# A four-layer recurrent-memory / hedgehog-attention kernel: feature weights multiplied into the query and key weights on the chip

## The chip, the cores and the metric

The kernel runs on one core of one Trainium2 chip. The metric is the device time in microseconds; the time given for a kernel is the median of its runs. Every detailed duration below comes from one profiled execution on that core, counted from the start of its span.

## What is computed

Two layer types alternate, A B A B, over an activation of 2048 rows by 640 columns. Layer A is a recurrent-memory attention over 64 segments of 32 rows; the change doesn't touch its mathematics. Layer B is a linear attention with 32 heads of 20 columns and a "hedgehog" feature map:

```python
qkv = (x @ wqkv)                       # x: normalised rows, 640 -> 3 x 640
q, k, v = ...                          # 32 heads, 20 columns each
pq = einsum('bhsd,hdf->bhsf', q, w_phi)
pk = einsum('bhsd,hdf->bhsf', k, w_phi)
phi_q = concat(softmax(pq), softmax(-pq))
phi_k = concat(softmax(pk), softmax(-pk))
kv = einsum('bhsf,bhsd->bhfd', phi_k, v)
z  = einsum('bhsf->bhf', phi_k)
num = einsum('bhqf,bhfd->bhqd', phi_q, kv)
den = einsum('bhqf,bhf->bhq', phi_q, z) + 1e-06
x = x + (num / den) @ wo
```

Both B layers use the same `wqkv`, `w_phi` and `wo`.

## The kernel before

**Layer A** (lines 582 to 1149) has a preparation (`A_pre`), in which TensorE (PE) works at full rate, and a chain of 64 segments (`A_chain`), each depending on the one before. Its instructions are ordered by hand. After the chain, `post_steps` multiplies the attention outputs of the last 8 rows of every segment by Wo, in four batches of 96 matmuls (`multiply`). Layer B's code calls it.

**Layer B** (`layer_B`, lines 249 to 550) is placed by a scheduler that works at build time: it decides the order of the instructions on each engine, and each engine then runs its own list in that order. An instruction whose inputs aren't ready blocks everything behind it on its engine. Layer B has these stages:

- *Start* (456 to 474). SP issues the loads of x, of the tail outputs and of the three 640-column parts of `wqkv`, in the order keys (j = 1), values (2), queries (0). The four `multiply` batches run on PE while the first rows are normalised (`norm_rows`, line 357: an addition on POOL, statistics on DVE, logarithm and exponential on ACT, scaling). `turn_rows` transposes normalised rows on PE into `xnT` and ACT copies them out of PSUM.
- *Loop* (476 to 489) over NG = 4 groups of 512 rows. `heads_T(xnT, 1, "kT")` computes the keys of the group, columns on partitions: six chunks of six heads (120 columns; the sixth has 40), each the sum of five matmuls of 512 columns. Each chunk is copied from PSUM to SBUF, five by ACT and the last by DVE. `keys_values` then takes the group's four blocks of 128 rows. For a block it multiplies the keys by `wbd`, a block-diagonal form of `w_phi` (seven small matmuls into two PSUM banks), takes exp and exp of the negative on ACT (line 407), sums them per head (410) and inverts the sums (412) on DVE. It computes the values with two times five matmuls of 320 columns (419), scales them on DVE (423) and adds to the running kv sums with twelve small matmuls (429). At the end of the group `heads_T(xnT, 0, "qT")` does for the queries what was done for the keys.
- `query_features` of a group runs one group later, and for the last group in the tail: six matmuls with `wbd` (439), twelve exponentials on ACT (441), twelve matmuls that sum them per head (445), reciprocals, and twelve times a spreading matmul (452) with a multiplication on DVE (453).
- *Tail* (490 to 550): masked copies of kv and its sums, then per group denominators, numerators, the output projection (533) and, in the first B layer, the next normalisation.

Ten names of PSUM tiles share a pool of three banks (`bank`, line 297). A second pool of two (`side_bank`) holds those of the query features and denominators. `late_constants` (317) fills constants on POOL and DVE and is placed at the second group's normalisation.

The loop, the part that the change rewrites most:

```python
keys_values(g, xnT)
if waiting is not None:
    query_features(*waiting)
waiting = (g, heads_T(xnT, 0, "qT"))
```

All large buffers are cut by hand from one `arena`. Addresses under LATE = 64512 hold in layer B among others `qTs`, `lgs`, `oTs`, `obs`; above it lie `wbd`, `wqkv`, `kTs`, `xnTs`, `vrs`, `x2`, `xns`. In layer A the same addresses hold weights, so that a load of A's weights waits for the B buffers that it overlaps.

## Time and profile before

| what | us |
|---|---|
| median of 3 runs (3726.93 to 3730.69) | 3728.3 |
| span of the profiled execution | 3735.3 |
| layer B, first time: first key matmul to first numerator | 1617.1 to 1777.5 |
| layer B, second time: first key matmul to first numerator | 3487.2 to 3643.2 |
| second layer A: first matmul of its preparation | 1881.7 |
| DMA of one 640-column part of `wqkv`, from issue to landing | 10.7 |

Over the whole span PE is busy 3543.7 us (95%), DVE 2368.0 (63%), ACT 2073.4 (56%) and POOL 1658.5 (44%). Most of that is layer A: its chain runs from about 169 to 1555 and from about 2045 to 3430. In the profile's rows PE means matmuls and PEld the loading of their stationary operand. "Idle before, releaser" says how long an engine stood before an instruction and what it waited for. Matmuls overlap in the pipeline, so the time that one more of them costs is the distance between starts, not the duration in its row: for the 512-column matmul the row says 379 ns, and thirty in a row start within 6.67 us, 222 ns apart.

### The profile page before, as it was taken

What the parts mean: (1) busy time and instruction counts of PE and PEld (TensorE: products, weight loads), DVE (VectorE), ACT (ScalarE), POOL (GpSimd) and SP (SyncE); (2) the same over time, 40 slices, a digit from 0 to 9 for tenths busy, and PEclk for the clock granted to TensorE, in tenths of its full rate; (3) what the DMA queues carried; (4) which work ended last, traced back from release to release, by engine and by line L of the source; (5) the groups of instructions that cost most, each with busy time, mean ns of one, the idle gap of its engine ahead of it and who ended that gap; (6) DMA issues with size and microseconds to landing.
All of it is one profiled execution on the core that took longest, in us unless ns stands there. A gap on an engine that the chain in (4) does not pass through costs nothing.

```text
span 3735.3 us, 169098 instructions
## 1 busy us (share of the span) xinstructions
PE 3543.7 (95%) x71082; PEld 2319.9 (62%) x71390; DVE 2368.0 (63%) x6330; ACT 2073.4 (56%) x5285; POOL 1658.5 (44%) x4323
## 2 busy tenths in 40 slices
PE   9999999999999999989899999999999999999898
PEld 7766666666666666545377666666666666665453
DVE  5556666666666666456633566666666666664564
ACT  2356566666666666545423566666666666665453
POOL 3345555555555555340423455455555555553400
PEclk9999999999999999989899999999999999999899
DMA  9988788888887888910377888887887888879100
GB/s 301 326 295 294 266 289 292 275 291 278 284 294 272 293 282 276 309 57 14 137 259 216 292 279 282 283 295 275 290 282 274 289 282 289 293 268 316 58 1 29
DMA packets 531381, 931.72 MB, mean 249 GB/s; under 512 B 141034, under 2 KB 298362, under 8 KB 530618
## 3 DMA queue, kind: packets, MB, share of 16 engines
q1 hardware_dynamic: 428794, 818.87, 62.6%
q0 software_dynamic: 68160, 88.78, 8.1%
q10 hardware_dynamic: 33664, 13.24, 1.4%
q8 instruction: 558, 9.14, 1.0%
q14 instruction: 205, 1.68, 0.1%
HBM read 852.43 MB, written 72.09 MB: 248 GB/s over the span
## 4 chain that ended last, share of the span: by engine, by line
PE 35%; DVE 5%; DMA 5%; ACT 4%; issue 4%; POOL 2%; PEld 2%; SPq 0%; POOLq 0%; DVEq 0%; ACTq 0%
PE ps_qk L926 9%; PE ps_w L1002 4%; PE ps_v L926 4%; PE ps_o L976 2%; PE ps_s L968 2%; PE ps_qk L389 2%; DMA arena<-wo_rows 2%; PE ps_pre L817 1%; PE ps_s L1034 1%; DVE hT L882 1%; PEld L817 1%; PE ps_s L963 1%; PE ps_idle L1009 1%; PE ps_v L419 1%; PE kv L429 1%
## 5 line engine op out<-in xcount | busy, mean ns | idle before, releaser
L926 PEld LDWEIGHTS <-hT 128*32 128x32 bf16 x30720 | 739.4, 96 | 433.1 <-DVE hT L1146 29.0
L926 PE MATMUL ps_qk<-arena,hT 128*32 128x384 bf16 x20480 | 996.3, 327 | 12.0 <-DMA arena<-in_A_Wk_dram 2.2
L936 ACT ACTIVATE raw<-ps_qk 128x384 bf16<-128x384 f32 x1024 | 503.1, 491 | 378.3 <-PE ps_s L1034 243.9
L1002 PE MATMUL ps_w<-arena,OT 128*32 128x160 bf16 x24576 | 542.7, 235 | 38.4 <-issue 22.1
L909 POOL DMA_DIRECT2D Vp<-vb x512 | 258.8, 506 | 661.6 <-PE ps_o L976 456.4
L926 PE MATMUL ps_v<-arena,hT 128*32 128x384 bf16 x10240 | 536.6, 329 | 6.6 <-DMA arena<-in_A_Wv_dram 6.6
L1002 PEld LDWEIGHTS <-OT 128*32 128x32 bf16 x24576 | 436.2, 97 | 131.1 <-issue 53.7
L941 DVE STREAM_TRANSPOSE KT<-raw 128x384 bf16<-128x384 bf16 x512 | 296.1, 578 | 195.9 <-ACT raw L936 191.9
L944 DVE STREAM_TRANSPOSE QT<-raw 128x256 bf16<-128x256 bf16 x512 | 227.9, 445 | 239.1 <-ACT raw L936 195.9
L897 POOL DMA_DIRECT2D kqb<-kqb x512 | 291.1, 569 | 173.3 <-POOL KT L905 148.2
L957 DVE CAST Vp<-ps_v 64x384 bf16<-64x384 f32 x512 | 286.2, 559 | 98.2 <-ACT Vp L955 82.7
L995 POOL DMA_DIRECT2D otb<-otb x512 | 283.0, 553 | 116.5 <-DVE otb L991 99.0
L955 ACT ACTIVATE Vp<-ps_v 64x384 bf16<-64x384 f32 x512 | 246.3, 481 | 154.2 <-PE ps_v L926 115.4
L982 DVE CAST OT<-ps_o 128x192 bf16<-128x192 f32 x512 | 183.2, 358 | 221.2 <-PE ps_o L976 203.1
L1041 DVE TENSOR_TENSOR E<-E,ps_s 80x320 bf16<-80x320 bf16 x512 | 247.5, 483 | 73.6 <-ACT ps_s L1040 69.5
L1020 ACT ACTIVATE E<-ps_s 80x320 bf16<-80x320 f32 x512 | 221.9, 433 | 126.1 <-PE ps_s L968 97.2
L976 PEld LDWEIGHTS <-Vp 80*128 80x128 bf16 x4096 | 184.3, 99 | 154.7 <-issue 120.6
L968 PE MATMUL ps_s<-QT,KT 128*80 128x80 bf16 (+1 forms) x3072 | 233.2, 213 | 24.3 <-DVE KT L941 13.4
L976 PE MATMUL ps_o<-E,Vp 80*128 80x80 bf16 x4096 | 234.5, 202 | 22.6 <-ACT Vp L955 4.2
L981 ACT ACTIVATE OT<-ps_o 128x192 bf16<-128x192 f32 x512 | 167.8, 328 | 152.6 <-PE ps_o L976 152.3
L890 ACT ACTIVATE Vp<-ps_w 32x160 bf16<-32x160 f32 x512 | 150.7, 294 | 175.0 <-DVE wt L1145 157.9
L968 PEld LDWEIGHTS <-KT 128*80 128x80 bf16 x3072 | 194.6, 119 | 73.5 <-issue 61.4
(152 smaller groups left out, 5462.5 us busy)
## 6 DMA issues: line engine op xcount, KB each, us to landing
arena<-wo_rows SPq DMA_DIRECT2D x792, 320.0 KB, 6.8
arena<-in_A_Wq_dram SPq DMA_DIRECT2D x427, 384.0 KB, 4.6
arena<-in_A_Wv_dram SPq DMA_DIRECT2D x427, 384.0 KB, 6.4
arena<-in_A_Wk_dram SPq DMA_DIRECT2D x768, 192.0 KB, 4.8
kqb<-kqb POOLq DMA_DIRECT2D x512, 48.0 KB, 5.1
arena<-in_A_Wk_dram SPq DMA_DIRECT2D x43, 384.0 KB, 7.1
vb<-arena POOLq DMA_DIRECT2D x128, 112.0 KB, 5.9
Vp<-vb POOLq DMA_DIRECT2D x512, 28.0 KB, 4.7
```

What stands on the lines that cost most here:

```text
L897: nc.gpsimd.dma_start(out=kqb[:], in_=self.kqb_d[s, :, r, :])
L909: nc.gpsimd.dma_start(out=Vs[n % 2][64:80, :], in_=self.vb_d[s, r].rearrange("g t f -> (g t) f"))
L926: nc.tensor.matmul(o[32 * g:32 * g + 32, 0:384], lhsT=hT[:, b, :], rhs=rhs, start=(i == 0), stop=(i == KC - 1), tile_position=(0, 32 * g), ...
L936: nc.scalar.activation(out=raw[:], in_=ps[:, 0:384], func=ACT.Copy)
L941: nc.vector.transpose(out=KT[:, :, 0:64], in_=raw[:, :].rearrange("p (c j) -> p c j", j=64))
L955: nc.scalar.activation(out=o, in_=i, func=ACT.Copy)
L957: nc.vector.tensor_copy(out=o, in_=i)
L968: nc.tensor.matmul(S[0:80, c0:c0 + 80 * (q1 - q0)], lhsT=KT[:, 3 * x + i, :], rhs=QT[:, x, q0:q1, :], start=False, stop=(x == 1 and i == 2 ...
L976: nc.tensor.matmul(O[x][:, 80 * i:80 * i + 80], lhsT=Vs[n % 2][0:80, 448 * x + k:448 * x + k + 128], rhs=E[0:80, 160 * x + 80 * e:160 * x ...
L995: nc.gpsimd.dma_start(out=self.otb_d[s, :, 96 * r:96 * r + 96], in_=otb[:, :, :].rearrange("p c t -> p (c t)"))
L1002: nc.tensor.matmul(W[32 * g:32 * g + 32, 0:160], lhsT=OT[:, c, q:q + 32], rhs=w[:, 640 * i + 160 * g:640 * i + 160 * g + 160], start=(firs ...
L1041: nc.vector.tensor_tensor(out=E[0:80, 0:320], in0=E[0:80, 0:320], in1=rc, op=ALU.mult)
```

## The change

The product (rows x Wq) x w_phi is computed as rows x (Wq x w_phi), and the same for the keys. A new function `fuse` makes the product of the weights on the chip in the first B layer, between the last `multiply` and the loop, and writes it over the query and key parts of `wqkv`. A DMA on POOL's queue keeps it in DRAM (`fused_d`), and the second B layer loads it from there in place of the raw weights. In the loop the key features then come from `xnT` directly, five matmuls of 320 columns for each half of a block; query features from the former query matmuls, with the exponentials reading their PSUM banks. `heads_T` is gone, and with it its copies and the buffers `qTs` and `kTs`. A smaller `wT` takes the place of `kTs`, which moves the buffers behind them. The features of a group's queries now belong to their own group; what is left of `query_features`, the normalisation, is `query_norms` and stays where it was.

```diff
-        qTs = self.views(take(2 * f4), f4, 2)
...
-        kTs = self.views(take(2 * f4), f4, 2)
+        wT = self.view(take(KC * NC_ * 256), KC * NC_ * 256).rearrange("p (k c m) -> p k c m", k=KC, c=NC_)
...
-            def heads_T(xnT, j, name):
...
+            def fuse(j):
+                for k in range(KC):
+                    pt = bank("ps_t", BF16)
+                    for c in range(NC_):
+                        self.transp(out=pt[0:sizes[c], P * c:P * c + P],
+                                    in_=wqkv[:, k, D * j + CH * c:D * j + CH * c + sizes[c]], identity=self.ident[:, :])
+                    full = P * (NC_ - 1)
+                    self.ev.copy(out=wT[0:CH, k, 0:NC_ - 1, :].rearrange("p c m -> p (c m)"), in_=pt[0:CH, 0:full])
+                    self.ev.copy(out=wT[0:sizes[-1], k, NC_ - 1, :], in_=pt[0:sizes[-1], full:full + P])
+                for k in range(KC):
+                    for c0, c1 in ((0, 3), (3, NC_)):
+                        ps = bank("ps_f")
+                        for c in range(c0, c1):
+                            mc, o = sizes[c], CH * (c - c0)
+                            nc.tensor.matmul(ps[:, o:o + mc], lhsT=wT[0:mc, k, c, :], rhs=wbd[0:mc, c, 0:mc], start=True,
+                                             stop=True)
+                        n = sum(sizes[c0:c1])
+                        self.ev.copy(out=wqkv[:, k, D * j + CH * c0:D * j + CH * c0 + n], in_=ps[:, 0:n])
+                nc.gpsimd.dma_start(out=self.fused_d[:, :, D * j:D * j + D], in_=wqkv[:, :, D * j:D * j + D])
 
             def keys_values(g, xnT):
-                kT = heads_T(xnT, 1, "kT")
...
-                        for c in range(NC_):
...
+                        for k in range(KC):
+                            nc.tensor.matmul(ps[:, 0:W2], lhsT=xnT[:, k, q:q + P],
+                                             rhs=wqkv[:, k, D + W2 * u:D + W2 * u + W2], start=(k == 0), stop=(k == KC - 1))
...
-            def query_features(g, qT):
+            def queries(g, xnT):
                 tk = slice(512 * g, 512 * g + 512)
                 for c in range(NC_):
                     mc = sizes[c]
-                    ps = side_bank("ps_pq")
-                    nc.tensor.matmul(ps[0:mc, :], lhsT=wbd[0:mc, c, 0:mc], rhs=qT[0:mc, c, :], start=True, stop=True)
+                    ps = bank("ps_pq")
+                    for k in range(KC):
+                        nc.tensor.matmul(ps[0:mc, :], lhsT=wqkv[:, k, CH * c:CH * c + mc], rhs=xnT[:, k, :],
+                                         start=(k == 0), stop=(k == KC - 1))
                     for sg in range(2):
                         nc.scalar.activation(out=phi[0:mc, sg, c, tk], in_=ps[0:mc, :], func=ACT.Exp, scale=1.0 - 2.0 * sg)
+
+            def query_norms(g):
...
             for j in (1, 2, 0):
...
+                src = self.B_wqkv.rearrange("(k p) n -> p k n", p=P) if j == 2 or self.fused_d is None else self.fused_d
+                nc.sync.dma_start(out=wqkv[:, :, D * j:D * j + D], in_=src[:, :, D * j:D * j + D])
...
             multiply(3, ow[3], kv_ps[1], side_bank("ps_post"))
+            if self.fused_d is None:
+                self.fused_d = self.dram.tile([P, KC, 2 * D], BF16, name="fused")
+                for j in (1, 0):
+                    fuse(j)
...
                 keys_values(g, xnT)
                 if waiting is not None:
-                    query_features(*waiting)
-                waiting = (g, heads_T(xnT, 0, "qT"))
+                    query_norms(waiting)
+                queries(g, xnT)
+                waiting = g
```

## The prediction

> **What bounds the kernel now.** I read the page first, then busy time by stretch. PE is busy 95% of the span, but nearly all of it is layer A, which the change leaves alone. What decides here are two stretches, 1617 to 1878 and 3487 to 3735. The stretches of the second B layer, one for each group of 512 rows and one for the tail (stretch, length, then busy time and instructions on PE, PEld, DVE, ACT, POOL, granted clock, DMA share, GB/s):

> ```profile
> 3485.00:3530.00 45.00, 35.23 (x216) 22.33 (x215) 23.89 (x54) 14.96 (x36) 18.38 (x38) 0.81 0.13 37
> 3530.00:3568.00 38.00, 34.70 (x226) 20.77 (x226) 26.10 (x48) 25.73 (x59) 2.60 (x8) 1.00 0.01 1
> 3568.00:3607.00 39.00, 35.30 (x226) 20.79 (x226) 24.63 (x40) 25.05 (x52) 1.87 (x4) 1.00 0.00 1
> 3607.00:3646.00 39.00, 35.99 (x216) 20.72 (x216) 27.44 (x68) 19.49 (x42) 1.88 (x4) 1.00 0.00 1
> 3646.00:3735.00 89.00, 73.28 (x332) 31.34 (x329) 42.62 (x82) 29.29 (x51) 8.70 (x16) 0.90 0.09 30
> ```

> PE is first with 35 of 38 us, DVE and ACT have 25, DMA nothing. To see how a group passes I read PE in order of time (start, length, engine, line; in brackets how long PE stood before it and for whom):

> ```profile
> 3531.01 6.74 PE L389 MATMUL ps_qk<-arena 128*120 128x512 bf16 x30 [1.13 <-ACT arena L89]
> 3537.68 0.44 PE L404 MATMUL ps_pk<-arena 120*128 120x120 bf16 x6
> ...
> 3541.64 0.41 PE L404 MATMUL ps_pk<-arena 120*128 120x40 bf16 x4 [0.77 <-ACT arena L407]
> ...
> 3553.89 1.03 PE L389 MATMUL ps_qk<-arena 128*120 128x512 bf16 x4
> ...
> 3568.46 6.74 PE L389 MATMUL ps_qk<-arena 128*120 128x512 bf16 x30 [1.11 <-ACT arena L89]
> ```

> A period is 37.45 us (3531.01 to 3568.46; the next is 38.78): 6.67 of keys in which PE works alone, 16.2 of blocks (to 3553.89), 14.6 of queries. DVE in order of time stands 7.6 us before the copy of the last key chunk (3537.79) and then runs nearly without a gap to 3567. So keys are bound by PE, blocks and queries by the round trip between PE, ACT and DVE.

> **Each matmul's price** is the distance of starts: 6.67/30 = 0.222 us at 512 columns; values at 320 columns 0.137 (ten from 3494.86 to 3496.23); six small feature matmuls 0.29 (3537.68 to 3537.97), so 0.05 each; a kv matmul 0.094 (ten from 3552.13 to 3553.07).

> **The loop, groups 1 to 3.** Out: 30 key matmuls 6.67, 28 small ones 1.4, six query-feature matmuls 1.3: 9.4 us. In: 40 of 320 columns, like the values: 5.5. Net 3.9 of PE in a group. ACT loses ten copies of 0.60, DVE two of 0.68; the exponentials stay. The twelve of the queries now read the query banks, 0.5 us apart (three in 1.61): two for each chunk, 1.0 us, against 1.11 for its five matmuls, so PE still sets the pace. They also read one of the three shared banks, which a copy held for half as long; I count 0.5 for that.
> Blocks, new: the first block's keys 1.37 and the exponentials 0.9 pass before DVE starts. Then a block costs the round trip: sum 1.48, reciprocal 0.55, first pair of products 0.89, five key matmuls of the next block 0.68, exponentials 0.77: 4.4, with 0.3 for handing over 4.7. Three of them and 2.9 for the last: 2.3 + 14.1 + 2.9 = 19.3; PE's own work there is 17.9 (keys 5.5, values 5.5, 36 kv 3.4, sums 2.7, some spreading 0.8), and the queries can start a little before DVE ends: 18.7. Queries, new: 6.67 + spreading 1.8 + kv 1.1 + transposes 1.3 = 10.9, plus 2.5 of waits (today 1.1 for ACT's copy of `xnT`; it now also stands behind the exponentials): 13.4. Period 32.1, 5.4 to 6.7 less than today. Bounds: 3.9 (stalls unchanged) and 6.7 (the whole key phase). I take 5.3. Six periods: **32 us** (23 to 40).

> **Group 0, second B layer.** The built order of the changed kernel puts the first block's keys directly behind the last post batch (3487.21). Today the first kv matmul is held by DVE, and DVE by an addition on POOL behind the late constants (they end at 3496.4). Now DVE reaches the second block's sum before its first such statistics; but the kv matmul needs POOL's cast of the reciprocals, which stands behind those constants: 3496.9. Against 3502.88 that is 6 gained instead of the 6.7 of keys. After that DVE needs 4.5 a block (its statistics among them): scaled values end near 3511 against 3520. That is up to 9.5 with the queries behind it; where PE stays at the half clock that it shows here today, its blocks set the pace again and 3 are left. I take **7** (3 to 9.5).

> **Group 0, first B layer: the fusion.** 60 transposes, 60 matmuls, 40 evictions: PE 0.066 each, 8 us in all; evictions half each on DVE and ACT. Nearest rows: 640-wide copy out of PSUM 0.48 on DVE, 384-wide 0.55 and on ACT 0.44 (320): about 0.43 apart. A half needs 5 + 5 on DVE, 4.5 us. DVE comes free of the last post output at 1620.65, so the keys' half ends near 1625.2. Then the order matters. The changed kernel has one bn_stats between the two halves on DVE, and it is the instruction that today stands here:

> ```profile
> 1629.27 0.89 DVE L221 BATCH_NORM_STATS2 ln_stats<-arena 128x6 f32<-128x320 bf16 x2 [4.70 <-POOL arena L361]
> ...
> 1634.28 0.46 PE L429 MATMUL kv<-arena 128*120 128x126 bf16 x2 [4.56 <-DVE arena L423]
> ```

> POOL's constants end at 1627.8 in both kernels and its addition at 1629.2, so DVE idles 4 us and the queries' half runs 1629.7 to 1634.6. PE's order puts the keys behind it. First sum 1638 against 1631.03; scaled values then follow DVE's 4.2 a block or PE's half clock: the next group starts 1666 to 1671 against 1663.77. I take **-4** (-14 to +2). The two stores (800 KB, 640 rows each; nearest row 0.54 for 128 rows, at most 2.7 us on POOL) stand ahead of two additions and the casts of the reciprocals, needed only near 1640: nothing. The second layer's loads are as long as before.

> **Tail.** The last group's six query matmuls (1.3) leave, and the built order lays six of twelve spreading matmuls between the output projection where today twelve follow each other at DVE's 0.6 us (3675.13 to 3682): 2.3. With ACT relieved **5** for both layers (2 to 7). A's weight loads wait on moved buffers: `obs` now holds a Q piece instead of a V piece, four places earlier in SP's queue. SP issues these pieces by 1900 and PE needs them from 1921: hidden; 5 us if not.

> Sum: 32 + 7 - 4 + 5 = **40 us** off the profiled span of 3735.3: 3695. That span lies 7 above the median of the runs, so 3728.3 - 40 = **3688**.

> [...] Row first: where PE stood 4.56 us (above), the stretch has a granted clock of 0.73 in the first B layer and 0.81 in the second, and kv matmuls start 0.147 apart instead of 0.094. In groups 1 to 3, with waits of at most 1.13, it is 1.00. [...] I follow the row.

> **Rivals.**
> 1. *The round trip takes the keys' place* (15%). If banks and hand-overs make a block 5.5: 2.3 + 16.5 + 2.9 = 21.7, queries as today 14.6: 36.3, 1.8 a period. 11 + 7 - 8 + 3 = 13: 3715. For it: DVE's gapless blocks. Against: 6.67 us without DVE work go.
> 2. *Slower: half clock in the blocks* (7%). PE's 17.9 becomes 36, the period 49, 17 over my forecast. It decides from the third such period on (40/17); all six give 3688 + 102 = 3790. For it: group 0 today; against: the three groups at 1.00.
> 3. *All goes* (11%): 7 a period, fusion hidden behind today's stall (+2), 9 and 7: 60: 3668.
> 4. *The change doesn't do what it says*: the order shows no key copies and loads from `fused_d`; under 1%, left out.

> **Numbers.** The forecast has 67%, its own range 3674 to 3703. Rivals 1 and 3 are faster too. With those inside, 3668 to 3714 leaves out the clock case and the outer edges. Within 0.2% (7.5 us, what this measurement can tell from none) is rival 1 gone further: 5%. Slower 8%: the clock and part of rival 1. Faster 87%.

> **What would show it.** Periods between `xnT`'s first key matmuls near 32 us at clock 1.00; DVE without the 7.6 us gap; in the first B layer a wait of 4 us of DVE on POOL's addition between two runs of copies; first kv matmul of the second B layer near 3497 minus what came off before. Wrong would be: periods over 36, a clock under 0.9 in groups 1 to 3, or an idle PE in the second A preparation after its first 20 us.

## The result and the profile after

The changed kernel takes 3735.69 us (median of 14 runs, 3725.2 to 3749.04); the kernel before, beside it, 3730.18 (14 runs, 3721.39 to 3741.97). The ratio is 1.0011, 95% interval 0.9998 to 1.0025: no change, where 3688 had been forecast. The profiled execution has a span of 3731.6 us against 3735.3.

A span that hardly moves can hide two large movements, so I cut it into stages by PE in order of time: from the first to the last `ps_w` matmul of each chain of layer A, and what lies between.

| stage, us of the profiled execution | before | after | difference |
|---|---|---|---|
| up to the first chain's first output matmul | 186.2 | 182.5 | -3.7 |
| first chain | 1373.1 | 1368.3 | -4.8 |
| first layer B and second preparation | 492.7 | 475.5 | -17.2 |
| second chain | 1375.1 | 1431.3 | **+56.2** |
| second layer B, to PE's last matmul | 298.6 | 264.3 | -34.3 |

Both B layers got faster, by 51.5 us in all. The second chain, whose instructions the change doesn't touch, took it back.

**The B layers went as forecast in kind.** Busy time by stretch in the second one, a stretch for each group (columns as before the prediction):

```profile
3517.00:3552.00 35.00, 28.27 (x192) 18.36 (x188) 20.44 (x45) 14.10 (x32) 16.41 (x34) 0.90 0.13 40
3552.00:3583.00 31.00, 29.12 (x201) 18.52 (x201) 24.21 (x45) 19.90 (x47) 2.71 (x6) 1.00 0.01 1
3583.00:3616.00 33.00, 30.81 (x209) 18.93 (x206) 22.90 (x40) 20.33 (x43) 1.87 (x4) 1.00 0.00 1
3616.00:3646.00 30.00, 28.12 (x179) 17.25 (x178) 23.79 (x48) 14.28 (x32) 1.87 (x4) 1.00 0.01 1
```

The granted clock stays at 1.00 in groups 1 to 3 with PE busy about 94% of each stretch. The periods are read from PE in order of time (start, length, engine, line):

```profile
3517.71 1.52 PE L411 MATMUL ps_pk<-arena 128*128 128x320 bf16 x10
...
3522.12 0.70 PE L411 MATMUL ps_pk<-arena 128*128 128x320 bf16 x4 [0.85 <-ACT arena L414]
3526.31 0.37 PE L436 MATMUL kv<-arena 128*120 128x126 bf16 x2 [3.48 <-POOL arena L422]
...
3552.03 1.53 PE L411 MATMUL ps_pk<-arena 128*128 128x320 bf16 x10
...
3583.32 0.97 PE L411 MATMUL ps_pk<-arena 128*128 128x320 bf16 x6
...
3615.82 1.38 PE L411 MATMUL ps_pk<-arena 128*128 128x320 bf16 x9
...
3645.61 0.43 PE L533 MATMUL ps_num<-arena 120*120 120x512 bf16 x1
```

Group 0 runs from 3517.71 to 3552.03; the next starts are 3583.32 and 3615.82, the first numerator (`ps_num`) 3645.61: periods of 31.3, 32.5 and 29.8 us where the kernel before has 37.45, 38.78 and 36.0. The first kv matmul of group 0 waits for POOL's cast of the reciprocals (3.48 us), as the prediction had it.

**What grew.** The waits of PE in the second chain, from 2050 to 3420 before and from 2030 to 3450 after (engine, tile or line waited at, releaser: us in all, times, longest; "issue" is time for which the profile shows no cause). The kernel before:

```profile
PE ps_w L1002 <- issue: 11.4, 18, 1.4
...
PEld L1002 <- issue: 24.3, 39, 1.8
...
PEld L926 <- issue: 5.7, 5, 3.0
```

The changed kernel (L943 and L1019 are the former L926 and L1002):

```profile
PE ps_v L943 <- issue: 36.2, 62, 1.5
...
PEld L943 <- issue: 83.1, 117, 2.7
...
PEld L1019 <- issue: 3.6, 8, 0.8
```

The weight loads of these two lines waited 30.0 us without a shown cause and now wait 86.7: 56.7 more, as much as the chain lost. (The other lines with such waits have much the same sums in both, 60 us at the sums of the exponentials for one.) PE in order of time shows where. In the changed kernel:

```profile
2505.39 1.01 PE L1019 MATMUL ps_w<-arena,OT 128*32 128x160 bf16 x48
2506.23 0.82 PE L943 MATMUL ps_v<-arena,hT 128*32 128x384 bf16 x14
2508.24 0.50 PE L943 MATMUL ps_v<-arena,hT 128*32 128x384 bf16 x6 [1.19 <-issue]
```

and the same place of a segment in the kernel before:

```profile
2513.80 1.01 PE L1002 MATMUL ps_w<-arena,OT 128*32 128x160 bf16 x48
2514.64 0.99 PE L926 MATMUL ps_v<-arena,hT 128*32 128x384 bf16 x20
```

Twenty value matmuls that form one run before are broken after the fourteenth, in the middle of a sum, where the profile shows nothing to wait for: no engine, no DMA of the program, no bank.

**What differs there**, in the chain's own instructions, is only the place in PE's list. The page's third part, queues, has two queues that carry instructions; the larger one (packets, MB, share), before:

```profile
q8 instruction: 558, 9.14, 1.0%
```

PE's list as built has 142,894 entries in the kernel before (matmuls, weight loads and what the profile doesn't count). 9.14 MB for them is 64 bytes each, and 142,894 / 558 is 256: the list comes in pieces of 256. In the trace each of the 558 packets is 16,384 bytes, 256 entries of 64. A segment of the chain is exactly 1024 entries, four pieces, so all 64 segments cross their borders at the same four instructions, and what a border costs there can be paid 64 times. Two lines of layer A's code set the place: `fill` issues empty weight loads ahead of each chain.

```python
FILL = {0: 86, 2: 78}
...
                if s == 0:
                    fill(FILL[li])
```

I call "remainder" the number, modulo 256 and counted from 0 in the list as built, of the entry that ends a chain's first segment. In the kernel before it is 165 for both chains. In the changed kernel the first layer B has 47 entries more ahead of the second chain: 165 for the first, **212** for the second.

### The profile page after: what moved, and what is told of

It reads as the page before. It is cut to its first block, busy times and chain, and to the rows that moved or that the text cites. A ratio compares the mean times of both kernels' runs of the same rounds, so it can differ in the third digit from the quotient of the medians.

```text
span 3731.6 us, 168901 instructions
## 1 busy us (share of the span) xinstructions
PE 3537.4 (95%) x71010; PEld 2312.5 (62%) x71318; DVE 2365.5 (63%) x6334; ACT 2038.1 (55%) x5225; POOL 1665.2 (45%) x4325
## 4 chain that ended last, share of the span: by engine, by line
PE 38%; DVE 6%; ACT 4%; issue 4%; DMA 2%; PEld 2%; POOL 2%; SPq 0%; POOLq 0%; DVEq 0%; ACTq 0%
PE ps_qk L943 10%; PE ps_v L943 5%; PE ps_w L1019 5%; PE ps_o L993 3%; PE ps_s L985 2%; DVE hT L899 2%; PE ps_s L1051 2%; PE ps_pq L447 2%; PE ps_s L980 1%; PEld L834 1%; PE ps_pre L834 1%; PE ps_idle L1026 1%; PE ps_v L426 1%; DVE E L1058 1%; ACT raw L953 1%
## 5 line engine op out<-in xcount | busy, mean ns | idle before, releaser
L943 PEld LDWEIGHTS <-hT 128*32 128x32 bf16 x30720 | 745.0, 96 | 507.0 <-issue 90.4
L943 PE MATMUL ps_qk<-arena,hT 128*32 128x384 bf16 x20480 | 1004.5, 328 | 14.8 <-DMA arena<-in_A_Wq_dram 2.8
L943 PE MATMUL ps_v<-arena,hT 128*32 128x384 bf16 x10240 | 569.0, 330 | 43.7 <-issue 36.2
L926 POOL DMA_DIRECT2D Vp<-vb x512 | 259.6, 507 | 716.9 <-PE ps_o L993 473.1
L1019 PE MATMUL ps_w<-arena,OT 128*32 128x160 bf16 x24576 | 533.1, 235 | 15.8 <-DMA arena<-wo_rows 9.5
L1019 PEld LDWEIGHTS <-OT 128*32 128x32 bf16 x24576 | 434.3, 97 | 101.6 <-issue 25.1
L985 PE MATMUL ps_s<-QT,KT 128*80 128x80 bf16 (+1 forms) x3072 | 233.4, 213 | 21.4 <-DVE KT L958 13.1
L919 POOL COPY QT<-kqb 128x64 bf16<-128x64 bf16 x512 | 126.5, 247 | 252.3 <-PE ps_s L985 244.1
```

What stands on the lines that cost most here:

```text
L926: nc.gpsimd.dma_start(out=Vs[n % 2][64:80, :], in_=self.vb_d[s, r].rearrange("g t f -> (g t) f"))
L943: nc.tensor.matmul(o[32 * g:32 * g + 32, 0:384], lhsT=hT[:, b, :], rhs=rhs, start=(i == 0), stop=(i == KC - 1), tile_position=(0, 32 * g), ...
L985: nc.tensor.matmul(S[0:80, c0:c0 + 80 * (q1 - q0)], lhsT=KT[:, 3 * x + i, :], rhs=QT[:, x, q0:q1, :], start=False, stop=(x == 1 and i == 2 ...
L1019: nc.tensor.matmul(W[32 * g:32 * g + 32, 0:160], lhsT=OT[:, c, q:q + 32], rhs=w[:, 640 * i + 160 * g:640 * i + 160 * g + 160], start=(firs ...
```

## The experiments

Theory P: the place in the list makes the loss. Theory D: the chain's loads and buffers, which the change moved (`obs` now holds a Q piece). A constant in `FILL` moves the place and otherwise only adds or takes away empty weight loads ahead of a chain. The kernel before was timed anew beside each group of experiments, with 3741.79 (e1 to e4), 3730.21 (e5 to e8) and 3736.51 us (e9, e10); across groups the ratios to it are compared.

**e1: the changed kernel, second chain back at 165.**

```diff
-FILL = {0: 86, 2: 78}
+FILL = {0: 86, 2: 31}
```

> The changed kernel with FILL[2] = 31 instead of 78: 47 fewer empty weight loads ahead of the second A chain, so that each of its 1024-instruction segments stands where it stood before in PE's instruction list, counted modulo 256. Theory P (the place in PE's list decides): the second chain takes 1545 us from the preparation's first matmul to the last output matmul instead of 1602, the time is 3735.7 - 56 = 3680, ratio 0.986. Rival D (the new DRAM buffer and the moved SBUF buffers slow the chain's weight loads): nothing changes, 3735.

3691.16 us (5 runs), ratio 0.9861 [0.9838, 0.9883]. The second chain takes 1383.6 us. Waits of PE in it:

```profile
PE ps_w L1019 <- issue: 9.2, 19, 1.3
```

Back where they were before, at `ps_w`, with about the former sum. P is borne out: 47 empty weight loads fewer are worth 1.5%.

**e2: the kernel before, second chain moved to 212.**

```diff
-FILL = {0: 86, 2: 78}
+FILL = {0: 86, 2: 125}
```

> The kernel before with FILL[2] = 125 instead of 78, nothing else: 47 more empty weight loads, which puts its second chain where the changed kernel has it. Theory P: the second chain becomes 56 us longer, 3786, ratio 1.015, with a PE wait of about 0.6 to 1.2 us in each segment in the value matmuls that the trace ascribes to nothing. Rival D: 47 empty loads, 1 to 4 us, 3733.

3797.15 us (4 runs), ratio 1.0149 [1.0124, 1.0174]; second chain 1430.8 against 1375.1. Waits of PE in it:

```profile
PE ps_v L926 <- issue: 39.3, 65, 2.2
```

The loss arises without the change, and at the value matmuls too.

**e3: the changed kernel, 256 entries further than e1** (`FILL[2]` = 287).

> The changed kernel with FILL[2] = 287 = 31 + 256. Theory P with a period of 256 instructions: the second chain is as in e1, plus 256 empty loads at 0.03 to 0.08 us: 3688 to 3700. If the period is longer (512 or 1024), the chain is somewhere else: any time, probably over 3710. Rival D: 3735 plus those loads, 3745.

3695.15 us (4 runs), ratio 0.9887 [0.9857, 0.9917], the interval overlapping that of e1, and the second chain takes 1372.6: the effect repeats after 256 entries. (In the profiles the stretch ahead of the chain is 7.6 us longer than in e1, 484.1 against 476.5, with 256 more loads in it.)

**e4: without the fusion.** Both B layers then use the raw weights and leave the multiplication with `w_phi` out; `FILL[2]` = 17 keeps the second chain at 165.

```diff
-            if self.fused_d is None:
-                self.fused_d = self.dram.tile([P, KC, 2 * D], BF16, name="fused")
-                for j in (1, 0):
-                    fuse(j)
```

> As e1, but the fusion is left out (FILL[2] = 17 for the same place in PE's list): the loop multiplies with the raw query and key weights in both B layers, so that w_phi is left out of the computation. What is missing against e1 is the fusion's price. The prediction's own terms (group 0 of the first layer -4, of the second +7): 11 us faster than e1, 3669. From the trace of the change (first B layer gained 17, second 34): 17 faster, 3663. If the fusion hid behind the wait of DVE for POOL that the first layer has anyway: as e1, 3680. Rival D: 3720 to 3735.

3678.77 us (4 runs), ratio 0.9831 [0.9804, 0.9858]: 12.4 us less than e1. The two intervals overlap, but each of the four runs is shorter than each of e1's five. In the profiles the second group of the first layer B starts 94.1 us after the chain's end, in e1 107.2: 13.1 us.

**e5: e1 with the fusion one projection batch earlier.**

```diff
             ow.append(spread(3, ot[3]))
+            if self.fused_d is None:
+                self.fused_d = self.dram.tile([P, KC, 2 * D], BF16, name="fused")
+                for j in (1, 0):
+                    fuse(j)
             multiply(2, ow[2], kv_ps[0], side_bank("ps_post"))
...
             multiply(3, ow[3], kv_ps[1], side_bank("ps_post"))
-            if self.fused_d is None:
-                self.fused_d = self.dram.tile([P, KC, 2 * D], BF16, name="fused")
-                for j in (1, 0):
-                    fuse(j)
```

> The changed kernel with the second chain's place in PE's list as in the kernel before (31 empty weight loads instead of 78), and with the fusion issued one matmul batch earlier, so that the third projection batch's matmuls and the row turns stand behind it instead of ahead of it. If the 12.4 us that the fusion costs (3691.2 against 3678.8 us without it) are PE's waits for the evictions and VectorE's wait for POOL's addition, the projection batch gives PE work during those waits and some 4 to 8 us come back: about 3685 us, 0.985 of the kernel before. If the fusion's cost is PE's and the two copying engines' own work, nothing comes back: 3691 us, 0.987. If the fused weights then reach the evictions' engines while these still copy projection rows, it gets 3 us slower: 3694 us.

3680.24 us (4 runs), ratio 0.9865 [0.984, 0.989]. Against e1's 0.9861 nothing comes back. The interval alone would leave room for some of the 4 to 8 us hoped for, but in the profiles the second group starts 107.6 us after the chain's end (107.2 in e1). PE in order of time:

```profile
1585.19 0.33 PE L398 MATMUL ps_f<-arena 120*128 120x120 bf16 x3
1598.00 1.26 PE L398 MATMUL ps_f<-arena 120*128 120x120 bf16 x9 [7.31 <-DVE arena L87]
```

Between the two rows other batches run; then PE stands 7.31 us for a copy on DVE. The keys of group 0 start 2.4 us earlier after the chain than in e1 (74.7 against 77.1), but the group doesn't end earlier. That the two evicting engines' work sets the 12 us fits this; it isn't shown by itself.

**e6: the changed kernel at remainder 37** (`FILL[2]` = 159).

> The changed kernel with 159 empty weight loads ahead of the second chain: 128 more than the 31 with which it took 3691.2 us. Theory: pieces of 256 instructions, each chain segment has four borders at fixed places, and the cost is set by where they fall. With 128 more the borders fall in the middle between the old ones; if the pieces were of 128 instructions or fewer the time would be that of 31 again, 3691 us (0.987). With pieces of 256 the borders fall on other work, and the time is another one: anything from 3685 to 3750 us, and not within 5 us of 3691 unless the second places cost as little.

3724.74 us (10 runs), ratio 0.9987 [0.9973, 1.0001]; second chain 1418.5. Half a period from e1 it is 1.3% slower: the period is 256, not 128 or a part of it.

**e7: the kernel before, first chain moved to 212, second left at 165.**

```diff
-FILL = {0: 86, 2: 78}
+FILL = {0: 133, 2: 31}
```

> The kernel before, with 47 more empty weight loads ahead of the first chain (133 instead of 86) and 47 fewer ahead of the second (31 instead of 78), so that the second chain stands where it stood and the first one has the place that the second has in the changed kernel. If the place alone makes the cost, the first chain gets 56 us longer, the second does not, and the time is 3728 + 56 = 3785 us, ratio 1.015. If the cost needs something that only the second chain has (what the feature layer leaves behind), there is no change: 3730 us, 1.000.

3785.2 us (4 runs), ratio 1.0148 [1.0118, 1.0178]. The first chain takes 1423.7 (1373.1), the second 1372.4. Waits of PE in the first chain:

```profile
PE ps_v L926 <- issue: 37.2, 58, 1.2
```

The line and about the count and the sum of the changed kernel's second chain, in a chain that no layer B precedes. What the feature layer leaves behind plays no part.

**e8: the changed kernel at remainder 189** (`FILL[2]` = 55).

> The changed kernel with 55 empty weight loads ahead of the second chain, between the 31 (3691.2 us) and the 78 (3735.7 us). If the cost grows evenly with the distance: 3691 + 24/47 x 44.5 = 3714 us. If it depends on whether a border falls inside the run of twenty value matmuls (it does from about 64 up), there is no cost yet at 55: 3691 us.

3714.28 us (one run), 1405.1 for the chain: about half the loss at half the distance.

**e9 and e10: the changed kernel at remainders 133 and 101** (`FILL[2]` = 255 and 223).

> The changed kernel with 255 empty weight loads ahead of the second chain (remainder 133 by 256, 32 less than the 165 of the kernel before). In all traces so far PE's unexplained waits in the chain sit at the instructions with remainder 193 or 194 by 256, whatever they are. Here these are, in each segment: the 11th of 20 ps_qk matmuls, two ps_s matmuls, and the 22nd of 48 ps_w matmuls. If the border makes the wait, any unexplained waits stand only there (a ps_w group broken after 21, 27 left; a ps_qk group broken with 10 left). Time: the border of 165 that still cost 10 us moves 32 instructions on, the cost falls by 10 us or another border takes over for up to 15 us: ratio 0.983 to 0.990, likeliest 0.984. If the waits belong to certain instructions and not to the place in the list: ps_v and ps_w groups broken where they were broken before (43, 23, 6, 2 left).

> The changed kernel with 223 empty weight loads ahead of the second chain (remainder 101 by 256). Borders by the same rule: the 7th of 20 ps_v matmuls, two places in ps_qk groups, and the 38th of 48 ps_w matmuls. Unexplained waits only there (a ps_v group with 14 left, a ps_w group with 11 left). The third border then lies between two measured places, one that cost nothing and one that cost 35 us: time between 0.986 and 0.997 of the kernel before, likeliest 0.991. If waits belong to certain instructions: groups broken where they were before, 43, 23, 6, 2 left.

e9: 3751.93 us (10 runs), ratio 1.0031 [1.0012, 1.005]. e10: 3737.49 us (10 runs), ratio 0.9997 [0.9981, 1.0014]. Both times were missed: 133 was to be the cheap place and is the dearest by its time. The places of the waits, all but single ones, are among those expected. PE in order of time in e9:

```profile
2392.63 0.58 PE L1019 MATMUL ps_w<-arena,OT 128*32 128x160 bf16 x21
2395.20 0.67 PE L1019 MATMUL ps_w<-arena,OT 128*32 128x160 bf16 x27 [1.98 <-issue]
```

in e10:

```profile
2622.67 0.86 PE L1019 MATMUL ps_w<-arena,OT 128*32 128x160 bf16 x37
2625.38 0.51 PE L1019 MATMUL ps_w<-arena,OT 128*32 128x160 bf16 x11 [1.85 <-issue]
```

in e6:

```profile
2509.93 0.66 PE L1019 MATMUL ps_w<-arena,OT 128*32 128x160 bf16 x25
2511.38 0.60 PE L1019 MATMUL ps_w<-arena,OT 128*32 128x160 bf16 x23 [0.79 <-issue]
```

in e8:

```profile
2906.04 0.34 PE L943 MATMUL ps_v<-arena,hT 128*32 128x384 bf16 x1
2907.02 0.51 PE L943 MATMUL ps_v<-arena,hT 128*32 128x384 bf16 x7 [0.64 <-issue]
```

A matmul and its weight load are two entries. In e9 the broken `ps_w` group begins at remainder 152, so 21 matmuls end at 152 + 42 = 194; in e10 it begins at 120, and 37 end at 194; in e6 at 143, 25 end at 193; in e8 the `ps_v` group begins at 192, one ends at 194; in the changed kernel the twenty values begin at 166, fourteen end at 194. Different instructions, one place: the border of a piece. That it lies at 194 of my count and not at 0 is read from these waits alone; what stands in the chip's list ahead of the kernel's entries isn't known.

**What PE waits for** is in the traces, which time each packet of that queue: 16,384 bytes, about 1.03 us from start to end. In the changed kernel, e9, e10, e6 and e8 the last packet ahead of the waits above ended at 2506.85, 2393.77, 2623.98, 2509.90 and 2905.39, and PE went on 1.39, 1.43, 1.40, 1.48 and 1.63 us later. In the second chains of all twelve traces 499 first matmuls behind a border waited without a shown cause; each went on 1.2 to 1.7 us after a packet's end, and none of the other 2540 came sooner than 1.2 us after one. So PE waits for the piece itself, at the borders that it reaches before that time is over.

| remainder | kernels | ratio to before | second chain, us | where the unexplained waits of matmuls stand |
|---|---|---|---|---|
| 165 | e1, e3 | 0.9861, 0.9887 | 1383.6, 1372.6 | 19 and 15 times with 43 of 48 `ps_w` left |
| 189 | e8 | 0.9957 (one run) | 1405.1 | 35 times with 7 of 8 `ps_v` left |
| 212 | the change | 1.0011 | 1431.3 | 45 times with 2 of 12, 17 times with 6 of 20 `ps_v` left |
| 37 | e6 | 0.9987 | 1418.5 | 50 times with 23, 24 times with 27 of 48 `ps_w` left |
| 101 | e10 | 0.9997 | 1433.0 | 56 times with 11 of 48 `ps_w` left |
| 133 | e9 | 1.0031 | 1431.3 | 55 times with 27 of 48 `ps_w` left, 28 times at `ps_s` |

Of the six places tried one is cheap, and it is the one that the kernel before had for both chains. In the changed kernel the packets for the two borders that stall (both in `ps_v` groups) end 4.7 and 3.8 us (medians) after PE has passed the border before, those for the other two 2.3 and 1.9. Why a piece's transfer starts late behind one border and early behind another, and so why 32 entries decide, stays open. What else shares the DMA engines at that moment was not varied.

**The better version** is e1: the change with the second chain at its old place, 1.4% faster than the kernel before.

## Why the prediction was wrong

**The step that failed** is the sentence at its start: "nearly all of it is layer A, which the change leaves alone". From it every term for layer A but its weight loads was left out of the sum. The instructions are left alone, their place in the list isn't: PE waits in most segments of the second chain for pieces of its list, and this term, put at nothing, measures +56.2 us. With the old place (e1) the change gives 1 - 0.9861 = 1.39% of 3730, 52 us (44 to 60), which agrees with the 51.5 us that the B layers gained in the profile. None of the rivals contained the cause; the slower one had another mechanism. That the B layers' 51.5 and the chain's 56.2 nearly cancel is chance.

Point by point, forecast and measured (from the chain's end to the start of group 1 for group 0):

| term | forecast | measured |
|---|---|---|
| groups 1 to 3, six periods | 32 (23 to 40) | 20.1 + 18.6 = 38.7 |
| group 0, second layer | 7 (3 to 9.5) | 9.4 |
| group 0, first layer, with the fusion | -4 (-14 to +2) | -3.9 |
| tails and the preparation behind the first | 5 (2 to 7) | 0.9 + 6.3 = 7.2 |
| sum of the B layers | 40 | 51.4 (51.5 from the rounded stages) |
| second chain of layer A | 0 | -56.2 |
| start and first chain (same code; in profiles with the first chain at 165 it takes 1368 to 1382) | 0 | 8.5 |

- *The loop.* Right in kind: the key phase goes, and the clock stays at 1.00, so the rival of the half clock (the kernel before was granted 0.50 from 3500 to 3505, in group 0) didn't occur: in both kernels groups 1 to 3 ran at 1.00, with waits of at most 1.13 us before and 0.96 us after. Too small in size: I took 5.3 us a period, 6.45 came, near the upper bound of 6.7.
- *The fusion.* On DVE in the changed kernel:

```profile
1618.16 0.53 DVE L87 CAST arena<-ps_f 128x360 bf16<-128x360 f32 x1 [0.23 <-PE ps_f L398]
1621.21 0.49 DVE L222 BATCH_NORM_STATS2 ln_stats<-arena 128x6 f32<-128x320 bf16 x1 [2.52 <-POOL arena L361]
1621.62 1.27 DVE L87 COPY arena<-ps_t 120x640 bf16<-120x640 bf16 x3
...
1632.48 1.49 DVE L417 TENSOR_REDUCE sk<-arena 128x64 f32<-128x1280 bf16 x1 [1.27 <-ACT arena L414]
```

The statistics stand between the two halves as forecast; the wait is 2.5 us, not 4. The addition came when forecast (1629.2 less the 8.6 us by which the chain ends earlier here is 1620.6), but the keys' half took DVE 6.2 us (1612.5 to 1618.7) and not 4.5: it stood four times for PE, 1.3 us in all, which the term left out. The first sum (last row) starts 3.1 us later than forecast (1638 less 8.6), and from there to group 1 it is 26.6 us where -4 had 29.8: that -3.9 meets -4 is in part luck. The fusion's price alone, 12.4 us in e4, fits the distance of my two group-0 terms, 7 and -4.
- *Group 0 of the second layer.* The first kv matmul starts 8.6 us after the layer's first key matmul instead of 15.7, held by POOL's cast as forecast.
- *Rival 3*, all goes, named 60 us; with 51.5 the truth for the B layers lies between it and the forecast.
- *The weight loads of A* cost nothing visible: the second chain of e5 takes 1373.4 us, as before.

The profile of before held a sign: 18 waits without a cause, 11.4 us in all, in the second chain, inside a run of matmuls that had its operands. With the count of PE's entries ahead of the chain (+47) it would have put layer A on the list of what can move.

## What to carry to other kernels

Where a long part of PE's list repeats with a period that is a multiple of a piece (here 1024 entries, four pieces of 256), every edit ahead of it can move it over the borders of the pieces (here 47 entries, 1.5%); compare its place before and after, and try the change at the old place before judging it. A wait without a cause, always at the same instruction of a run, is the mark of it, and it is confirmed where a packet of the instruction queue ends a fixed time (here 1.2 to 1.7 us) ahead of the wait's end. A small result of a large change is read stage by stage: here -51.5 and +56.2 us made up a difference of nothing.
